# Turning the attention's output on TensorE in the last two units, and the order of the products for the new values

## The chip, the cores and the metric

One core of a Trainium2 chip runs the whole program. The metric is the device time of one execution in microseconds, as the median of several runs. The core's engines work side by side, each through an instruction list of its own: TensorE (matmuls and transposes, results into PSUM), VectorE, ScalarE, GpSimd, and SyncE, which here only issues DMAs.

## What is computed

Three steps follow each other: a linear attention whose state is corrected by a delta rule, a dense network of two layers, and a routed network with eight experts of which each token takes one.

```python
# attention: q, k, v of (4, 8, 768, 48), beta of (4, 8, 768)
for t in range(S):
    y[:, :, t] = np.einsum('bhd,bhde->bhe', q[:, :, t], state)
    v_old = np.einsum('bhde,bhd->bhe', state, kt)
    state = state + bt[:, :, :, None] * np.einsum('bhd,bhe->bhde', kt, vt - v_old)
x = y.transpose(0, 2, 1, 3).reshape(3072, 384)
# dense network
h = x @ w_in
x = np.maximum(0.01 * h, h) @ w_out
# routed network
e_idx = np.argmax(x @ w_gate + modality_bias[modality_id], axis=1)
out[mask] = gate_w[mask, None] * (np.maximum(x[mask] @ w1[e], 0.0) @ w2[e])
```

## The kernel before

**Units.** The attention is cut into 12 units, numbered `u["i"]` from 0 to 11. A unit holds 128 tokens of two batches, that is 16 heads; 6 units follow each other in time for the first two batches and 6 for the other two. Within a unit the recurrence is replaced by matrix products: `gram` multiplies keys and queries, `base` and `merge` build the inverse of a triangular 128x128 matrix for each head, and `step` takes the state through the unit. Every float32 operand is kept as two float16 halves, a high and a low one, and a product is three matmuls: high by high, high by low, low by high (`P3`).

**The inverse and the new values.** The last step of `merge`, `d2(q)`, makes the inverse of four heads: VectorE writes it as `r1`, ScalarE casts the high half `mh`, and GpSimd subtracts to get the low half `ml` (L445). `q` runs from 0 to 3, so the last piece holds heads 12 to 15. `new` in `step` multiplies the inverse by the right side `R` and gives the new values `U`: two PSUM tiles `pu`, one for the even heads (`hh` 0) and one for the odd, with 8 heads of 3 matmuls each (L495). `carry` then updates the state, and `seen` forms the unit's output: PSUM tiles `py`, from which ScalarE casts the high half of `X` and VectorE subtracts the low one (L539). Together they are the tile `x`, tokens by 384 columns for two batches and two halves.

**The dense network.** `moe1(u)` works on the 256 tokens of a unit. It needs `x` with the columns on the partitions. `turn` makes that tile, `xt` (one buffer): for unit 0 by twelve TensorE transposes into two PSUM tiles `pxt` and two VectorE copies, for all others by two DMA transposes that SyncE issues (L709). After `turn` come eight steps `up` (L724, 18 matmuls each into a PSUM tile `ph`; two such buffers, which `pxt` shares), `up2` (ScalarE and VectorE write the two halves of `gt`, L735 and L736) and `down` (L746, 12 matmuls each into `po`). The last `down` ends in `x1`, which goes to the DRAM table `x1d` (L754), and in the gate's logits `lg` (L755).

**The order.** From unit 2 on, TensorE, ScalarE, GpSimd and SyncE keep the order in which the program is written; VectorE's order is chosen by a scheduler, and so are all orders in the opening (units 0 and 1). The loop over units hands out slots: in slot `n` it runs one piece of the dense network of the unit before, then the attention's pieces of that slot. The turn of a unit is put ahead of what is still left of the unit before, which is one `down`:

```python
if n == OFF - 1:
    fs = net.moe1(U[i])
    m = fs[:1] + m + fs[1:]
```

In units 1 to 9 the slots after `seen` also hold the pieces `prod` of a unit two further on; units 10 and 11 have none.

**The end.** `route` turns the logits into table rows and scatters them (GpSimd, `tb`, L850), `plan` counts the blocks of each expert, and `block` works on 256 tokens of one expert: SyncE loads `info` and the weights `wf` (L964), GpSimd gathers the tokens `xg` from `x1d`, ScalarE and VectorE split both into halves (L625, L626), TensorE turns the tokens (`pet`, L998) and multiplies (`eh` L1009, `eo` L1024). Three blocks are planned before the last two units are counted and start as soon as unit 11's dense network is through.

Of the kernel before, what the change touches and what calls it, by code (L numbers as in the profile page):

```python
# [62 lines left out]
class Net:  # L63
# [385 lines left out]
    def step(self, u):  # L449
        nc = self.nc  # L450
# [3 lines left out]
        P3 = ((0, 0), (0, 1), (1, 0))  # L454
# [33 lines left out]
        def new():  # L488
            M, R, U = [u["mh"], u["ml"]], st["R"], st["U"]
            pu = [self.ps.tile([128, 8, 48], F32, tag="ps", name=f"pu{hh}") for hh in range(2)]  # L490
            for hh in range(2):
                for p in range(8):
                    n = 2 * p + hh
                    for i, (a, b) in enumerate(P3):
                        nc.tensor.matmul(pu[hh][:, p], M[a][n // 8][:, n % 8, :], R[b][:, n, :],  # L495
                                         start=(i == 0), stop=(i == 2))
                nc.scalar.activation(hp(U[0], hh), pu[hh], ACTF.Copy, scale=1.0 / ST)
                nc.vector.scalar_tensor_tensor(out=hp(U[1], hh), in0=pu[hh], scalar=1.0 / ST, in1=hp(U[0], hh),
                                               op0=ALU.mult, op1=ALU.subtract)
# [19 lines left out]
        def seen():  # L519
# [22 lines left out]
            u["x"] = [[X[i][:, 8 * o:8 * o + 8].rearrange("p n d -> p (n d)") for i in range(2)] for o in range(2)]  # L542

        return [old, new, carry, seen]

    def setup_moe(self):
# [152 lines left out]
    def moe1(self, u):  # L699
        nc = self.nc  # L700
        g, c = u["g"], u["c"]
        P3 = ((0, 0), (0, 1), (1, 0))
        st = {}

        def turn():
            xt = st["xt"] = self.m2.tile([128, 2, 2, 3, 128], F16, tag="xt", name="xt", bufs=1)
            if u["i"]:
                for i in range(2):
                    nc.sync.dma_start_transpose(out=xt[:, i].rearrange("p t d n -> p (t d) n"), in_=u["xx"][i])  # L709
                return  # L710
            for t in range(2):
                pt = self.pm.tile([128, 2, 3, 128], F16, tag="ph", name="pxt")
                for i in range(2):
                    for d in range(3):
                        nc.tensor.transpose(pt[:, i, d], u["x"][t][i][:, d * 128:(d + 1) * 128], self.id16)
                nc.vector.tensor_copy(xt[:, :, t], pt)

        def up(f2):
            xt = st["xt"]
            ph = self.pm.tile([128, 2, 256], F32, tag="ph", name="ph")  # L720
            for ff in range(2):
                f = 2 * f2 + ff
                for i, (a, b, d) in enumerate((a, b, d) for b in range(2) for d in range(3) for a in range(2 - b)):
                    nc.tensor.matmul(ph[:, ff], self.win[a][:, d, f * 128:(f + 1) * 128], xt[:, b, :, d, :],  # L724
                                     start=(i == 0), stop=(i == 8))
            s = SG / (SX * SW)
            tl = self.m2.tile([128, 2, 256], F32, tag="tl", name="tl")
            nc.scalar.activation(tl, ph, ACTF.Copy, scale=0.01 * s)  # L728
            nc.vector.scalar_tensor_tensor(out=tl, in0=ph, scalar=s, in1=tl, op0=ALU.mult, op1=ALU.max)  # L729
            st["t", f2] = tl  # L730

        def up2(f2):
            tl = st.pop(("t", f2))
            G = st["g", f2] = self.m2.tile([128, 2, 2, 256], F16, tag="gt", name="gt")
            nc.scalar.copy(G[:, 0], tl)  # L735
            self.pace = nc.vector.tensor_tensor(out=G[:, 1], in0=tl, in1=G[:, 0], op=ALU.subtract).ins  # L736

        def down(f2):
            if f2 == 0:
                st["po"] = [self.pm.tile([128, 392], F32, tag="po", name=f"po{t}") for t in range(2)]  # L740
            po, G = st["po"], st.pop(("g", f2))
            for ff in range(2):
                f = 2 * f2 + ff
                for t in range(2):
                    for i, (a, b) in enumerate(P3):
                        x = nc.tensor.matmul(po[t], G[:, a, ff, t * 128:(t + 1) * 128], self.wout[b][:, f, :],  # L746
                                             start=(f == 0 and i == 0), stop=(f == 15 and i == 2))
            self.pace = x.ins
            if f2 == 7:
                for t in range(2):  # L750
                    x1 = self.m2.tile([128, 392], F32, tag="x1", name="x1")
                    nc.scalar.activation(x1, po[t], ACTF.Copy, scale=1.0 / (SG * SW))
                    r = (2 * g + t) * self.S + c * 128
                    nc.sync.dma_start(out=self.x1d[r:r + 128, :], in_=x1[:, :384])  # L754
                    nc.vector.tensor_copy(self.lg[:, 2 * (g * self.NC + c) + t, :], x1[:, 384:])  # L755

        w = lambda f, x: lambda: f(x)
        none = lambda: None
        r = [(turn, none), (w(up, 0), w(up2, 0)), (w(up, 1), w(up2, 1))]
        for f2 in range(8):  # L760
            r.append((w(down, f2), none))
            if f2 < 6:
                r.append((w(up, f2 + 2), w(up2, f2 + 2)))
        return r
# [510 lines left out]
```

## Time and profile before

| | us |
|---|---|
| median of 3 runs | 969.84 (966.62 to 973.54) |
| the profiled execution | 967.95 |
| its span, first to last instruction | 966.1 |

| engine | busy us | share |
|---|---|---|
| TensorE, matmuls | 849.6 | 88% |
| TensorE, weight loads | 642.4 | 66% |
| VectorE | 732.9 | 76% |
| ScalarE | 527.1 | 55% |
| GpSimd | 531.8 | 55% |

Weight loads run beside matmuls. A share is an average over the opening, the units and the experts' blocks; what a wait costs is read at its own place. The mean granted clock of TensorE is 0.976 of full speed.

### The profile page before, as it was taken

How to read it: one execution, taken by the hardware profiler on the slowest of the kernel's cores; microseconds unless marked ns; L12 is line 12 of the kernel's file. 1: busy time of each engine (PE TensorE's matmuls, PEld its weight loads, DVE VectorE, ACT ScalarE, POOL GpSimd, SP SyncE). 2: the span in 40 equal slices, each digit the busy share in tenths (PEclk: the TensorE clock that was granted, in tenths of full speed). 3: DMA queues.
4: the chain of work that ended last, by engine and by line, in shares of the span. 5: the costliest groups of instructions: out<-in, count | busy, mean ns of one | idle time of the engine just before them, and what ended most of it. 6: DMA issues, size and time to landing. Idle time of an engine off the chain costs nothing. (4 is left out here: it accounts for less than half of the span.)

```text
span 966.1 us, 26359 instructions
## 1 busy us (share of the span) xinstructions
PE 849.6 (88%) x10914; PEld 642.4 (66%) x10914; DVE 732.9 (76%) x1391; ACT 527.1 (55%) x915; POOL 531.8 (55%) x723
## 2 busy tenths in 40 slices
PE   2555789899999999999999999898989889999994
PEld 1434667677767777777777676676767667777773
DVE  7999789786878787878878696984667766767671
ACT  4666586465645555556555554443445455665551
POOL 3537558568585868686867676652413424242321
PEclk9999998799999999999999999999999989999998
DMA  8447544235537281928281827132075567777750
GB/s 224 122 118 167 116 108 119 48 76 94 109 55 147 44 159 28 173 30 172 31 168 14 169 31 139 26 57 46 3 216 138 189 229 223 258 230 240 243 170 20
DMA packets 316501, 119.47 MB, mean 124 GB/s; under 512 B 281851, under 2 KB 298660, under 8 KB 316372
## 3 DMA queue, kind: packets, MB, share of 16 engines
q1 hardware_dynamic: 306676, 95.55, 44.3%
q10 hardware_dynamic: 5760, 12.59, 4.0%
q0 software_dynamic: 3936, 9.57, 2.8%
q8 instruction: 87, 1.43, 0.6%
q14 instruction: 42, 0.34, 0.1%
HBM read 85.99 MB, written 19.07 MB: 109 GB/s over the span
## 5 line engine op out<-in xcount | busy, mean ns | idle before, releaser
L746 PE MATMUL po<-wouth,gt 128*128 128x392 f16 x768 | 209.0, 334 | 6.4 <-DVE gt L736 6.3
L724 PE MATMUL ph<-xt,winh 128*128 128x256 f16 x1152 | 207.7, 275 | 6.7 <-DMA xt<-x 6.7
L746 PEld LDWEIGHTS <-gt 128*128 128x128 f16 x1152 | 107.9, 99 | 81.4 <-DVE gt L736 11.1
L724 PE MATMUL ph<-xt,winl 128*128 128x256 f16 x576 | 138.5, 275 | 0.0
L746 PE MATMUL po<-woutl,gt 128*128 128x392 f16 x384 | 127.9, 333 | 0.0
L724 PEld LDWEIGHTS <-winh 128*128 128x128 f16 x1152 | 113.5, 99 | 20.0 <-DMA xt<-x 2.9
L729 DVE SCALAR_TENSOR_TENSOR tl<-ph,tl 128x512 f32<-128x512 f32 x96 | 65.8, 685 | 52.9 <-ACT tl L728 52.7
L736 DVE TENSOR_TENSOR gt<-tl,gt 128x512 f16<-128x512 f32 x96 | 84.8, 883 | 21.9 <-ACT gt L735 19.5
L1009 PE MATMUL eh<-ext,wah 128*128 128x256 f16 (+1 forms) x624 | 98.5, 266 | 2.5 <-DVE ext L999 2.5
L1030 POOL DMA_INDIRECT out_dram<-ob,info x25 | 25.6, 1026 | 123.2 <-ACT ob L1029 119.2
L728 ACT ACTIVATE tl<-ph 128x512 f32<-128x512 f32 x96 | 56.9, 593 | 64.3 <-PE ph L724 63.8
L735 ACT CAST gt<-tl 128x512 f16<-128x512 f32 x96 | 59.2, 617 | 57.4 <-DVE tl L729 55.9
L279 DVE SCALAR_TENSOR_TENSOR blf<-pg,betas,up 128x256 f32<-128x256 f32 x192 | 79.6, 475 | 7.8 <-PE pg L273 7.0
L289 POOL TENSOR_TENSOR bl<-blf,bh 128x512 f16<-128x512 f32 x48 | 57.8, 1204 | 48.8 <-ACT bh L288 48.6
L1009 PE MATMUL eh<-ext,wal 128*128 128x256 f16 (+1 forms) x312 | 80.7, 266 | 0.0
L445 POOL TENSOR_TENSOR ml<-r,mh 128x512 f16<-128x512 f32 x48 | 59.7, 1252 | 18.3 <-ACT mh L444 17.9
L318 POOL TENSOR_TENSOR t<-t,tmp 128x15 f32<-128x15 f32 (+4 forms) x165 | 61.4, 372 | 12.9
L1009 PEld LDWEIGHTS <-wah 128*128 128x128 f16 x624 | 58.6, 98 | 14.9 <-issue 5.2
L1024 PE MATMUL eo<-wbh,egh 128*128 128x384 f16 (+1 forms) x200 | 66.0, 330 | 0.0
L1024 PE MATMUL eo<-wbl,egh 128*128 128x384 f16 (+1 forms) x200 | 66.0, 330 | 0.0
L1024 PE MATMUL eo<-wbh,egl 128*128 128x384 f16 (+1 forms) x200 | 66.0, 330 | 0.0
L724 PEld LDWEIGHTS <-winl 128*128 128x128 f16 x576 | 56.9, 99 | 11.6 <-issue 4.4
(324 smaller groups left out, 2166.2 us busy)
## 6 DMA issues: line engine op xcount, KB each, us to landing
wf<-in_moe_w_dram SPq DMA_DIRECT2D x52, 768.0 KB, 4.6
x<-in_moe_w_in_dram ACTq DMA_DIRECT2D x24, 256.0 KB, 3.7
x<-in_moe_w_out_dram ACTq DMA_DIRECT2D x16, 384.0 KB, 3.0
bd<-bh SPq DMA_DIRECT2D x12, 512.0 KB, 3.8
t<-td SPq DMA_DIRECT2D x12, 512.0 KB, 4.9
r<-td SPq DMA_DIRECT2D x12, 512.0 KB, 7.1
k<-in_k_dram SPq DMA_DIRECT2D x24, 192.0 KB, 3.7
q<-in_q_dram SPq DMA_DIRECT2D x24, 192.0 KB, 4.3
```

Source lines behind the costliest of these rows:

```text
L279: nc.vector.scalar_tensor_tensor(out=f[:, :, 2 * pp + hh], in0=pg[hh][:, pp], scalar=self.betas[:, c, g * 16 + n:g * 16 + n + 1], in1=self ...
L289: nc.gpsimd.tensor_tensor(out=l, in0=f[:, i], in1=h, op=ALU.subtract)
L318: eng.tensor_tensor(out=t[:, j + 1:16, 0:j + 1], in0=t[:, j + 1:16, 0:j + 1], in1=tv, op=ALU.subtract)
L445: nc.gpsimd.tensor_tensor(out=u["ml"][o][:, qs], in0=r1, in1=u["mh"][o][:, qs], op=ALU.subtract)
L724: nc.tensor.matmul(ph[:, ff], self.win[a][:, d, f * 128:(f + 1) * 128], xt[:, b, :, d, :], start=(i == 0), stop=(i == 8))
L728: nc.scalar.activation(tl, ph, ACTF.Copy, scale=0.01 * s)
L729: nc.vector.scalar_tensor_tensor(out=tl, in0=ph, scalar=s, in1=tl, op0=ALU.mult, op1=ALU.max)
L735: nc.scalar.copy(G[:, 0], tl)
L736: self.pace = nc.vector.tensor_tensor(out=G[:, 1], in0=tl, in1=G[:, 0], op=ALU.subtract).ins
L746: x = nc.tensor.matmul(po[t], G[:, a, ff, t * 128:(t + 1) * 128], self.wout[b][:, f, :], start=(f == 0 and i == 0), stop=(f == 15 and i == 2))
L1009: nc.tensor.matmul(ph[:, ff], W[a][:, d, f * 128:(f + 1) * 128], xt[:, b, d, :], start=(d == 0 and i == 0), stop=(d == 2 and i == 2))
L1024: nc.tensor.matmul(po[t], G[a][:, ff, t * P:(t + 1) * P], W[b][:, f, :], start=(f == 0 and i == 0), stop=(f == 7 and i == 2))
```

## The change

In `new`, the loop over the halves of the inverse moves outside the loop over the heads: for each of the two PSUM tiles, 16 matmuls with `mh` come first and 8 with `ml` follow. The start flag is set on the first matmul of a tile only, where before each head had one, and the stop flag on the last. In `turn`, the DMA transposes remain for units 1 to 9; units 10 and 11 take the way of unit 0, TensorE transposes and VectorE copies. Lines below the first edit are one higher in the changed kernel.

```diff
             for hh in range(2):
-                for p in range(8):
-                    n = 2 * p + hh
-                    for i, (a, b) in enumerate(P3):
-                        nc.tensor.matmul(pu[hh][:, p], M[a][n // 8][:, n % 8, :], R[b][:, n, :],
-                                         start=(i == 0), stop=(i == 2))
+                for a in range(2):
+                    for p in range(8):
+                        n = 2 * p + hh
+                        for b in range(2 - a):
+                            nc.tensor.matmul(pu[hh][:, p], M[a][n // 8][:, n % 8, :], R[b][:, n, :],
+                                             start=(p == 0 and a + b == 0), stop=(p == 7 and a == 1))
...
         def turn():
             xt = st["xt"] = self.m2.tile([128, 2, 2, 3, 128], F16, tag="xt", name="xt", bufs=1)
-            if u["i"]:
+            if 0 < u["i"] < 10:
                 for i in range(2):
                     nc.sync.dma_start_transpose(out=xt[:, i].rearrange("p t d n -> p (t d) n"), in_=u["xx"][i])
                 return
```

TensorE's list before, in unit 10, from the end of `seen` (`py`) over the last two `down` steps (`po`) to the first `up` (`ph`):

```order
L536 MATMUL py_12246<-uh,ll 128x48
L746 LDWEIGHTS gt
L746 MATMUL po_11500<-wouth,gt 128x392
...
L746 MATMUL po_11501<-wouth,gt 128x392
L724 LDWEIGHTS winh
L724 MATMUL ph<-xt,winh 128x256
```

The same place in the changed kernel, from the end of one `down` step over the twelve transposes to the next `down`:

```order
L747 LDWEIGHTS gt
L747 MATMUL po_11501<-wouth,gt 128x392
L716 LDWEIGHTS x
L716 MATMUL pxt<-id_88,x 128x128
...
L747 LDWEIGHTS gt
L747 MATMUL po_11500<-wouth,gt 128x392
```

The transposes stand between the last two `down` steps, 12 matmuls on either side; in unit 11 it is the same.

SyncE's queue before, from unit 10's turn (the first DMA_TRANSPOSE; `t` and `r` are the inverse's parts for unit 11) to the first load of a plan (`ei`):

```order
L329 DMA r_12054<-td_399 128x16x128
L709 DMA_TRANSPOSE xt<-x 128x6x128 x2
L176 DMA v<-in_v_dram 128x8x48 x2
L754 DMA x1d<-x_12383 128x384
L754 DMA x1d<-x_12387 128x384
L709 DMA_TRANSPOSE xt<-x 128x6x128 x2
L754 DMA x1d<-x_13259 128x384
L754 DMA x1d<-x_13263 128x384
L947 TENSOR_LOAD ei_13294
```

And in the changed kernel:

```order
L329 DMA r_12054<-td_399 128x16x128
L176 DMA v<-in_v_dram 128x8x48 x2
L755 DMA x1d<-x_12397 128x384
L755 DMA x1d<-x_12401 128x384
L755 DMA x1d<-x_13287 128x384
L755 DMA x1d<-x_13291 128x384
L948 TENSOR_LOAD ei_13322
```

Four transposes are gone from the queue, and nothing else in it has moved.

VectorE's list before, in unit 11, from the second low half of `X` (L539) to the first routing step on the new logits (L796; the rows between are constants of the routing):

```order
L539 SCALAR_TENSOR_TENSOR x<-py_13131,x 128x8x48
L838 TENSOR_TENSOR r_off<-r_off,cnt 128x8
L883 TENSOR_SCALAR p_pick<-io_404 1x8
L896 TENSOR_SCALAR p_val<-io_404 1x8
L925 TENSOR_SCALAR p_tk<-iok 1x19
L755 COPY lg<-x_13259 128x8
L755 COPY lg<-x_13263 128x8
L796 TENSOR_TENSOR r_l<-lg,biast 128x16
```

And in the changed kernel:

```order
L540 SCALAR_TENSOR_TENSOR x<-py_13145,x 128x8x48
L839 TENSOR_TENSOR r_off<-r_off,cnt 128x8
L884 TENSOR_SCALAR p_pick<-io_404 1x8
L897 TENSOR_SCALAR p_val<-io_404 1x8
L926 TENSOR_SCALAR p_tk<-iok 1x19
L717 COPY xt<-pxt 128x2x384 x2
L756 COPY lg<-x_13287 128x8
L756 COPY lg<-x_13291 128x8
L797 TENSOR_TENSOR r_l<-lg,biast 128x16
```

The two copies of the turned tile stand ahead of the logits; the rest keeps its order. In unit 10 they stand directly behind the two L540.

## Rows read from the trace of the kernel before

**Rows 1.** The page, part 1: busy time, share of the span, instructions

```profile
PE 849.6 (88%) x10914; PEld 642.4 (66%) x10914; DVE 732.9 (76%) x1391; ACT 527.1 (55%) x915; POOL 531.8 (55%) x723
```

**Rows 2.** Who waited for whom, whole run: total us, times, longest

```profile
PE pu L495 <- POOL ml L445: 7.1, 12, 1.4
...
PE ph L724 <- DMA xt<-x: 6.7, 2, 4.2
```

**Rows 3.** Timeline, TensorE, unit 10: start, us, what [idle before <-releaser]

```profile
649.11 0.33 PE L746 MATMUL po<-wouth,gt 128*128 128x392 f16 x1
...
657.46 0.37 PE L724 MATMUL ph<-xt,winh 128*128 128x256 f16 x1 [4.22 <-DMA xt<-x]
...
660.94 0.63 PE L356 MATMUL px<-t,bm 128*128 128x64 f16 x16
661.41 0.27 PE L724 MATMUL ph<-xt,winh 128*128 128x256 f16 x1
...
663.37 0.40 PE L365 MATMUL pz<-xp,r 128*128 128x64 f16 x8
```

**Rows 4.** Windows: PE, PEld, DVE, ACT, POOL busy, PEclk, DMA share, GB/s

```profile
656.00:662.00 6.00, 4.54 (x40) 3.46 (x40) 0.17 (x1) 0.80 (x2) 0.00 (x0) 0.72 0.58 120
...
709.00:739.00 30.00, 30.00 (x236) 22.13 (x235) 21.48 (x46) 15.68 (x23) 7.35 (x8) 1.00 0.70 210
```

**Rows 5.** Timeline, TensorE, unit 11

```profile
698.50 0.33 PE L746 MATMUL po<-wouth,gt 128*128 128x392 f16 x1
...
705.16 0.39 PE L724 MATMUL ph<-xt,winh 128*128 128x256 f16 x1 [2.53 <-DMA xt<-x]
...
712.63 0.33 PE L746 MATMUL po<-wouth,gt 128*128 128x392 f16 x1
```

**Rows 6.** Timeline, VectorE: the low halves of X in units 10 and 11

```profile
649.96 1.01 DVE L539 SCALAR_TENSOR_TENSOR x<-py,x 128x384 f16<-128x384 f32 x2
...
700.16 0.56 DVE L539 SCALAR_TENSOR_TENSOR x<-py,x 128x384 f16<-128x384 f32 x1
```

**Rows 7.** Transposes on TensorE: the experts' (timeline), unit 0's (line and tile views)

```profile
730.51 0.33 PE L998 MATMUL pet<-id,exh 128*128 128x128 f16 x3
...
731.18 0.27 PE L724 MATMUL ph<-xt,winh 128*128 128x256 f16 x1
...
L715 PE MATMUL pxt<-id,x x12: 219/219/314, 120.9 to 121.7; 128*128 128x128 f16 x12
...
L716 DVE COPY xt<-pxt x2: 547/552/558, 121.8 to 122.3; 128x768 f16<-128x768 f16 x2
```

**Rows 8.** Timeline, the wait for the last piece of ml before unit 10's new values

```profile
642.31 1.16 POOL L445 TENSOR_TENSOR ml<-r,mh 128x512 f16<-128x512 f32 x1 [0.32 <-ACT mh L444]
...
643.53 0.20 PE L495 MATMUL pu<-r,ml 128*128 128x48 f16 x1 [0.16 <-POOL ml L445]
```

**Rows 9.** Who waited for whom, TensorE, from 100 to 150 us (unit 0)

```profile
PE pu L495 <- POOL ml L445: 3.3, 4, 1.4
```

**Rows 10.** Timeline, unit 11: ScalarE, VectorE and TensorE towards the last down

```profile
714.82 0.62 ACT L735 CAST gt<-tl 128x512 f16<-128x512 f32 x1 [1.23 <-PE po L746]
...
736.36 0.69 DVE L736 TENSOR_TENSOR gt<-tl,gt 128x512 f16<-128x512 f32 x1 [0.74 <-ACT gt L735]
...
739.12 0.38 PE L1009 MATMUL eh<-ext,wah 128*128 128x256 f16 x2
```

**Rows 11.** Waits and timeline: the loads of the first expert's weights

```profile
SPq L947 <- DVE e_c L771: 0.5, 1, 0.5
...
704.07 0.18 DVE L771 TENSOR_SCALAR e_c<-r_l 128x32 f32<-128x32 f32 x1
...
706.04 2.33 SPq L964 DMA_DIRECT2D wf<-in_moe_w_dram  x4
...
715.34 1.48 ACT L625 ACTIVATE wah<-wf 128x1536 f16<-128x1536 f32 x1
```

**Rows 12.** The chain that ended last, its last gather

```profile
767.02 7.68 DMA xg<-x1d,idx
```

## The prediction

> **What bounds the kernel now.** I read the page first: TensorE is busy 849.6 us, 88% of the span, and no other engine passes 76% [rows 1]. So the question is where TensorE stands still in the two places that the diff touches, and whether the end of the program follows it. The waits of TensorE show both places by name [rows 2]: `up` waits 6.7 us for the transposed `xt`, in two waits only, and the products of `new` wait 7.1 us in 12 waits for the low half `ml` that GpSimd makes.
>
> The timeline shows the two waits for `xt`. In unit 10 the `down` matmuls start at 649.11 and end at 653.24; then TensorE is idle for 4.22 us, until 657.46 [rows 3]. In unit 11 the idle time is 2.53 us, before 705.16 [rows 5]. Units 1 to 9 show no such wait; there the matmuls of `gram` stand between. The idle time has a tail: the 18 matmuls of the first `up` of unit 10 take 657.46 to 660.94, 3.48 us, and the 18 of the next take 661.41 to 663.37, 1.96 us [rows 3]. The granted clock says why: 0.72 on average from 656 to 662, against 1.00 from 709 to 739 [rows 4]; it lay at the lower level (1.2 GHz) after the idle stretch and then rose to 2.4 GHz.
>
> **The turn of unit 10.** The four DMA transposes leave SyncE's queue; 24 TensorE transposes and 4 copies on VectorE come in. On TensorE they stand between the last two `down` steps. Twelve transposes of the same shape and type (L998) take 730.51 to 731.18, 0.67 us [rows 7]. Twelve `down` matmuls take half of 649.11 to 653.24 less a tail, 2.0 us. So: `down` 6 ends at 649.11 + 2.0 = 651.1. The low half of X is written from 649.96 for 1.01 us, to 650.97 [rows 6], so the transposes find their input and end at 651.8. `down` 7 ends at 653.8. Meanwhile VectorE copies the two PSUM tiles in 0.55 us each [rows 7], done by about 653.0, under `down` 7. If that cover were gone, 1.2 us would show. `up` starts at 653.8 instead of 657.46: **3.65 us**. Without the idle time the clock should not fall: another 3.48 - 1.96 = **1.5 us**. Unit 10 gives 5.15 us, and the work behind it in this unit hangs on TensorE and shifts with it.
>
> **The turn of unit 11.** `down` 6 runs 698.50 to 700.5 [rows 5]. Here VectorE is later: the second low half runs 700.16 to 700.72 [rows 6], so TensorE waits some 0.3 us, with 12 `down` matmuls queued behind the waiting transpose; whoever needs their results (ScalarE for `x1`, VectorE for the logits) gets them 0.9 us later than now. Transposes to 701.4, `down` to 703.4, `up` at 703.4 instead of 705.16: 1.75 us. The three `up` steps take 705.16 to 712.63, 7.47 us, against 3 x 1.96 = 5.88: 1.6 us for the clock. That makes 3.35 us on TensorE alone.
>
> Not all of it lasts. From the third `up` on, ScalarE and VectorE run one chain of `gt` and of the first expert's weights, with hardly a gap: ScalarE's cast at 714.82 follows `down`, and the last `gt` is ready at 736.36 + 0.69 = 737.05 [rows 10]. TensorE needs it 12 matmuls (2.0 us) before 739.12, at 737.1. There is 0.1 us of room, so TensorE can be no earlier than this chain. Its front is held by VectorE's small routing steps, which start on logits that are now 0.9 us later; stepping those rows on by hand I estimate the chain 3.0 us earlier, not 3.35. A second hold: SyncE waits for one of these steps (L771, at 704.07) before it issues the weights at 706.04, four loads at once; ScalarE casts the first at 715.34 without having waited [rows 11]. In unit 11's own time the cast is wanted 3 us earlier and the load is issued 0.9 us later. I take 0.3 us for it. Unit 11 gives **2.7 us**; bounds 0 and 3.35.
>
> **The new values.** All 16 products with `mh` now precede the 8 with `ml` in each half. One unit shows the place: TensorE waits 0.16 us until 643.53, for the last of four pieces of `ml`, which GpSimd starts at 642.31 [rows 8]. That piece belongs to the last four heads, whose first `ml` product was the 21st matmul of its half and is now the 23rd. So only 2 matmuls, some 0.025 us apart, move ahead of the wait, and 2 instead of 4 are left behind it: 0.05 us a unit. Of the 7.1 us, 3.3 in 4 waits lie in unit 0 [rows 9], where the scheduler mixes the two halves and TensorE waits for VectorE directly after. The other eight waits at 0.05 us: **0.4 us**, and 0 to 1.3 as bounds (the upper one if each wait shrinks by the 0.15 us of six matmuls). The start flag is now set once for a PSUM bank; that has no instruction of its own. The order of ScalarE's and VectorE's steps in the opening changes at two places by an instruction or three, which I cost at nothing, plus or minus 0.5 us.
>
> **What lies behind.** The end follows TensorE: after 739.12 the chain goes over the last `down`, the logits, the routing, the table and the last gathers, as the one at 767.02 that takes 7.68 us [rows 12]. Each of these starts on a result of the step before, not at a fixed time, so I let the whole gain through. SyncE is spared the issue of four transposes ahead of `v` and `x1d`; no wait for these shows, so I count nothing.
>
> **Sum.** 5.15 + 2.7 + 0.4 = 8.25 us. The profiled execution took 967.95 us (its span is 966.1), so it would take 959.7. The median of the three timed runs is 969.84, 1.9 us above it, and less 8.25 gives 961.6. I take the point between, a base of 968.9, and predict 960.6 us, 0.85% less.
>
> **Rivals.** (a) *The weights or VectorE hold unit 11.* The load for the cast at 715.34 lands some time before that; if it lands just before, nearly 3 us of unit 11 are given back, and unit 10's 5.15 and 0.4 are left: 963.3 us. For it speaks that four loads are issued together; against it that the first had 9.3 us to land [rows 11].
>
> (b) *The transposes are dear or don't keep the clock up.* The only transposes of this kind in the trace (L715, unit 0) start between 120.9 and 121.7 and last 0.22 us: 1.0 us for twelve, 0.35 more than I took [rows 7]. If the clock fell after them as it does now after the wait, both tails of 1.5 us would stay. Then 3.65 + 1.75 - 0.7 + 0.4 = 5.1 us and 963.8. Against it: twelve L998 transposes took 0.67 us in a stretch with clock 1.00 [rows 4, 7]. The Trainium skill, page "TensorE: Matmul & The Clock Gate", section "Part 4: PE-mode transpose", speaks for it: it gives about 275 ns for one transpose inside a kernel and says that transposes do not count as activity for the clock. An estimate from that page is 12 x 0.275 = 3.3 us a unit, which would leave some 3 us of the sum; the rows of L998 do not agree with it.
>
> (c) *Slower: TensorE stands before the transposes.* They stand in TensorE's own order now, with `down` behind them. If VectorE's X came later by d, all of TensorE would be d later, where the DMA let it go on. Today X is ready 0.1 us before TensorE arrives in unit 10 and 0.2 us after in unit 11 [rows 6]. The change breaks even when d is about 4 us in both units; at 6 us the time would be about 973. VectorE's order has only one `gt` subtraction and a few small steps ahead, so I see no source for 4 us.
>
> (d) *More than I count.* If `new` gives its upper bound, unit 11 its 3.35 and the later stretches close up as well, 10.3 us are saved: 958.6.
>
> **How the numbers follow.** Forecast 65% (959 to 962.5), (a) 15%, (b) 7%, (c) 3%, (d) 10%. Medians of this kernel scatter by some 0.3% (its three runs span 966.62 to 973.54), and about 1% is what can be told from no change. The 1% line lies at 9.7 us saved: (d) is beyond it, and scatter puts about a third of the forecast and a tenth of (a) and (b) there. That is 0.34 faster by over 1%, 0.62 within, 0.04 slower. The range for 8 in 10 takes in (a), (b), (d) and half a percent of scatter at either end: 954 to 968.
>
> **What the profile after would show.** No wait for DMA `xt` in units 10 and 11; transposes of about 0.67 us between the two `down` steps; clock 1.00 through both `up` steps; from the start of `down` 6 to the start of `up` 4.7 us in unit 10 (now 8.35) and 4.9 in unit 11 (now 6.66); `new`'s waits smaller by 0.05 us, not gone. I am wrong if TensorE shows a wait of over 1 us before the transposes or before the first expert's weights, or if the wait before the last gather grows by what was won.

## The result, and the profile after

Over 17 runs of each kernel the median went from 972.96 us to 965.16 us; the ratio is 0.991, with a 95% interval of 0.9887 to 0.9934. The medians lie 7.8 us apart; by the ratio it is 8.75 us less (6.4 to 11), where the sum was 8.25. Two of its terms did not go as they were written, though, and the step from the turn to the end held only in some of the traces.

The profiled execution of the changed kernel took 967.48 us (span 965.8), while that of the kernel before took 967.95. The two traces are 0.5 us apart where the medians are about 8 us apart, so the traces are read stretch by stretch here, not by their ends. One reason shows at once: at the start of unit 10's `down` 6, ahead of the first turn that was changed, the changed kernel's trace is already 3.23 us behind (652.34 against 649.11). Over all the traces of this document this start lies between 646.39 and 653.41 us; what makes it differ was not looked into. The page of the changed kernel, part 1, answers to [rows 1]:

```profile
PE 851.7 (88%) x10938; PEld 643.0 (67%) x10938; DVE 735.1 (76%) x1395; ACT 526.5 (55%) x915; POOL 534.6 (55%) x723
```

TensorE has 24 instructions more, VectorE four. The timeline of TensorE in unit 10 of the changed kernel, to be laid beside [rows 3]:

```profile
652.34 0.33 PE L747 MATMUL po<-wouth,gt 128*128 128x392 f16 x1
...
654.32 0.83 PE L716 MATMUL pxt<-id,x 128*128 128x128 f16 x12
...
654.99 0.33 PE L747 MATMUL po<-wouth,gt 128*128 128x392 f16 x1
...
656.98 0.27 PE L725 MATMUL ph<-xt,winh 128*128 128x256 f16 x1
...
658.95 0.63 PE L356 MATMUL px<-t,bm 128*128 128x64 f16 x16
```

No bracket stands behind `ph`: the wait of 4.22 us is gone. The twelve transposes take 654.32 to 654.99, 0.67 us. From the start of `down` 6 to the first `up` it is 4.64 us (forecast 4.7, before 8.35), and the first `up` takes 1.97 us to the work behind it (before 3.48). The same for unit 11, to be laid beside [rows 5]:

```profile
697.47 0.33 PE L747 MATMUL po<-wouth,gt 128*128 128x392 f16 x1
...
699.46 0.83 PE L716 MATMUL pxt<-id,x 128*128 128x128 f16 x12
...
702.12 0.27 PE L725 MATMUL ph<-xt,winh 128*128 128x256 f16 x1
...
708.24 0.33 PE L747 MATMUL po<-wouth,gt 128*128 128x392 f16 x1
```

Here it is 4.65 us to the first `up` (forecast 4.9, before 6.66), and the three `up` steps take 6.12 us (before 7.47). VectorE's copies of the turned tile, from the timeline, start under the last `down`:

```profile
654.86 1.02 DVE L717 COPY xt<-pxt 128x768 f16<-128x768 f16 x2 [0.73 <-PE pxt L716]
...
699.99 1.02 DVE L717 COPY xt<-pxt 128x768 f16<-128x768 f16 x2 [0.17 <-PE pxt L716]
```

They end at 655.88 and 701.01, 1.1 us before `up` wants them. The windows over both stretches (TensorE, its weight loads, VectorE, ScalarE, GpSimd busy, then the granted clock) answer to [rows 4]:

```profile
650.00:662.00 12.00, 12.00 (x232) 9.86 (x226) 6.04 (x13) 5.44 (x12) 7.12 (x7) 1.00 0.19 38
703.00:745.00 42.00, 41.93 (x332) 31.40 (x330) 33.02 (x101) 22.33 (x30) 12.45 (x12) 1.00 0.64 191
```

TensorE is busy for all 12 us of the first and the clock stays at 2.4 GHz (1.00, where 0.72 stood). For `new`, who waited for whom on TensorE, first in unit 0 (100 to 150 us, [rows 9] before), then from 150 to 700 us:

```profile
PE pu L496 <- ACT mh L444: 2.9, 2, 2.3
PE pu L496 <- POOL ml L445: 0.5, 1, 0.5
...
PE pu L496 <- POOL ml L445: 3.2, 4, 0.8
PE pu L496 <- ACT mh L444: 1.0, 4, 0.3
```

In unit 0, 3.4 us stand where 3.3 stood. Behind it, 4.2 us stand where [rows 2] less [rows 9] leave 3.8. The short waits are gone; four longer ones remain, each split into 0.3 us for `mh` and 0.8 for `ml`.

What unit 11 won did not stay, though. TensorE starts the first expert's matmuls (`eh`) at 734.74, 4.38 us before [rows 10]; at the second expert's first matmuls only 0.97 us of this lead are left. The timeline of the second expert's gather in the changed kernel shows where it went (GpSimd issues the gather `xg` in two parts, VectorE splits weights in `wal`, ScalarE casts the gathered tokens in `exh`):

```profile
739.58 1.69 DVE L627 SCALAR_TENSOR_TENSOR wal<-wf,wah 128x1536 f16<-128x1536 f32 x1
739.77 2.43 POOL L983 DMA_INDIRECT xg<-x1d,idx  x1 [5.51 <-ACT egh L1014]
...
742.50 1.96 POOL L983 DMA_INDIRECT xg<-x1d,idx  x1 [0.30 <-issue]
...
747.09 0.52 ACT L626 ACTIVATE exh<-xg 128x384 f16<-128x384 f32 x1 [2.34 <-DMA xg<-x1d,idx]
...
750.12 0.52 ACT L626 ACTIVATE exh<-xg 128x384 f16<-128x384 f32 x1 [2.51 <-DMA xg<-x1d,idx]
```

The first part starts 0.19 us after a split has begun and takes 2.43 us. In the trace before, it started at 743.93, 0.04 us ahead of the split, and took 1.05 us; the second part took 1.28:

```profile
743.93 1.05 POOL L982 DMA_INDIRECT xg<-x1d,idx  x1 [5.44 <-ACT egh L1013]
743.97 1.75 DVE L626 SCALAR_TENSOR_TENSOR wal<-wf,wah 128x1536 f16<-128x1536 f32 x1
...
745.29 1.28 POOL L982 DMA_INDIRECT xg<-x1d,idx  x1 [0.30 <-ACT wah L625]
```

The gather started 4.16 us earlier than there, and its last tokens were cast only 0.97 us earlier. Added up, the changed kernel's trace was 3.23 us behind at unit 10, won 5.22 us there, lost 0.96 us on the way to unit 11, won 3.35 us by the first `eh` and lost 3.41 us at the second expert: 0.97 us. The chain that ended last shows the third expert's gather as it was, to be laid beside [rows 12]:

```profile
766.09 7.65 DMA xg<-x1d,idx
```

Two questions were left for experiments: what each part of the change is worth, and whether the lead is lost by chance or always.

### The profile page after: what moved, and what is told of

Same layout as the page of the kernel before. It is cut to its first block, busy times and chain, and to the rows that moved or that the text cites. A ratio compares the mean times of both kernels' runs of the same rounds, so it can differ in the third digit from the quotient of the medians.

```text
span 965.8 us, 26397 instructions
## 1 busy us (share of the span) xinstructions
PE 851.7 (88%) x10938; PEld 643.0 (67%) x10938; DVE 735.1 (76%) x1395; ACT 526.5 (55%) x915; POOL 534.6 (55%) x723
## 5 line engine op out<-in xcount | busy, mean ns | idle before, releaser
L725 PE MATMUL ph<-xt,winh 128*128 128x256 f16 x1152 | 204.7, 273 | 0.1
L725 PE MATMUL ph<-xt,winl 128*128 128x256 f16 x576 | 136.3, 273 | 0.0
L318 POOL TENSOR_TENSOR t<-t,tmp 128x15 f32<-128x15 f32 (+4 forms) x165 | 63.6, 386 | 12.9
L444 ACT CAST mh<-r 128x512 f16<-128x512 f32 x48 | 29.5, 617 | 61.1 <-DVE r L442 61.1
```

Of the source, the lines that this page charges most:

```text
L318: eng.tensor_tensor(out=t[:, j + 1:16, 0:j + 1], in0=t[:, j + 1:16, 0:j + 1], in1=tv, op=ALU.subtract)
```

## The experiments

Fourteen traces bear on the explanation. The table puts them side by side; its numbers are differences of start times in the timelines. "Unit 10" is the time from `down` 6 to the second `up`, "unit 11" from `down` 6 to the `down` behind three `up` steps. "Gather to split" is the start of the second expert's gather on GpSimd less that of the VectorE split nearest to it; the two times behind it are how long the gather's parts took to issue. The lead is how much earlier than in the first trace TensorE began the first, second and third expert's `eh` (for the third, the step that stands at 785.94 there). A lead also holds what a trace had won or lost ahead of unit 10, so compare the three leads within a row, not one lead between rows.

| kernel, trace | unit 10 | unit 11 | gather to split, parts | third `idx` | lead at 1st, 2nd, 3rd |
|---|---|---|---|---|---|
| before, first | 12.30 | 14.13 | -0.04: 1.05, 1.28 | 1.87 | 0 |
| before, second | 11.90 | 15.81 | -0.20: 1.05, 1.37 | 1.87 | -1.5, -1.5, -1.5 |
| order in `new` alone | 11.24 | 15.10 | -0.10: 1.05, 1.27 | 0.23 | -1.2, -1.2, 4.9 |
| unit 11 alone | 12.07 | 10.99 | -0.29: 1.05, 1.45 | 0.23 | 1.1, 1.5, 7.5 |
| unit 10 alone | 7.94 | 11.66 | -0.20: 1.05, 1.37 | 0.23 | 2.6, 2.7, 8.7 |
| turn alone | 7.94 | 10.99 | +0.31: 2.30, 1.96 | 0.23 | 5.6, 3.0, 9.2 |
| changed, first | 7.08 | 10.77 | +0.19: 2.43, 1.96 | 1.87 | 4.4, 1.0, 0.7 |
| changed, second | 7.08 | 10.77 | -0.41: 1.05, 1.58 | 1.87 | 8.3, 8.7, 8.8 |
| split one slot later | 7.08 | 10.76 | -0.92: 1.05, 2.17 | 1.87 | 10.3, 8.6, 8.4 |
| transposes last | 8.09 | 11.76 | -0.25: 1.05, 1.42 | 1.87 | 6.8, 7.2, 7.0 |
| split two slots later | 7.08 | 10.77 | -1.84: 1.06, 0.97 | 1.88 | 7.9, 7.4, 6.8 |
| all units turned | 7.08 | 10.76 | -0.48: 1.05, 1.65 | 1.87 | 4.5, 4.9, 5.2 |
| both tiles' `mh` first | 7.08 | 10.77 | -0.53: 1.05, 1.70 | 1.87 | 10.0, 10.5, 9.9 |
| third split later | 7.08 | 10.77 | -0.31: 1.05, 1.49 | 0.23 | 11.1, 11.6, 14.6 |

**The turn alone.** The kernel before with the second edit only:

```diff
-            if u["i"]:
+            if 0 < u["i"] < 10:
```

> The kernel before with the second edit alone: units 10 and 11 are turned on TensorE, the products of new keep their old order. Theory (the sum: unit 10 5.15, unit 11 2.7 to 3.35, new 0.4): 7.8 to 8.5 us less than before, ratio 0.9912 to 0.9919; from the start of the next to last down to the first up 4.65 us in both units, no wait for xt. Rival 1 (the order in new carries the change, in units that no row of the two traces shows): less than 4 us here, ratio above 0.996. Rival 2 (the turn is worth the whole, and new is worth nothing or costs): 8.75 us or more, ratio 0.991 or less. In the trace, where its last gather lands decides how much of the 8 us is left at the end: theory 8, rival 3 (the last experts' gathers do not follow) 4 to 5.

Measured: 960.01 us against 966.84 for the kernel before, ratio 0.9938 (0.9912 to 0.9964), 6.0 us. The theory's 0.9912 to 0.9919 lies at the edge of the interval; rival 1 (above 0.996) lies at the other edge, with 0.9964 as the end of the interval, and the second (0.991 or less) is just outside. The trace speaks against rival 1: with the turn alone, units 10 and 11 take 7.94 and 10.99 us (before 12.30 and 14.13). In this trace rival 3 was at work: of a lead of 5.6 us, 3.0 were left at the second expert, whose gather met a split (timeline):

```profile
738.36 1.69 DVE L626 SCALAR_TENSOR_TENSOR wal<-wf,wah 128x1536 f16<-128x1536 f32 x1
...
738.67 2.30 POOL L982 DMA_INDIRECT xg<-x1d,idx  x1 [5.63 <-ACT egh L1013]
```

Unit 10 took 7.94 us instead of 7.08 here. ScalarE stood 1.27 us before it cast the second half of X, VectorE's low half came later by that, and TensorE waited in the middle of the transposes (timeline of the same trace):

```profile
650.04 0.49 ACT L538 ACTIVATE x<-py 128x384 f16<-128x384 f32 x1 [1.27 <-remote]
...
651.17 0.68 PE L715 MATMUL pxt<-id,x 128*128 128x128 f16 x9 [0.25 <-DVE x L539]
```

This is the forecast's rival (c) at a small scale: X came about 1.3 us later, and `down` and `up` behind the transposes came 0.86 us later with it.

**The order in `new` alone.** The kernel before with the first edit only (the diff of the change, its first part).

> The kernel before with the first edit alone: in new, all products with the high half stand ahead of those with the low half; the turn is left to the DMA in units 10 and 11. Theory: 0.4 us less (0 to 1.3), ratio 0.9987 to 1.0; TensorE's waits for ml before the new values sum to 6.5 to 7 us, against 7.1. Rival 1 (the order carries the change): 3 us or more, ratio 0.997 or less. Rival 2 (the order costs, since the 1.1 to 3 us that the changed kernel's trace had lost by unit 10 came from it): 1 to 3 us more, ratio 1.001 to 1.003.

Measured: 965.36 us, ratio 0.9983 (0.9962 to 1.0003), 1.6 us less with an interval that takes in zero and 0.4. Rival 2 (1.001 or more) is outside, and the 3 us of rival 1 lie inside the interval but near its end. TensorE's waits for `ml` before `new` sum to 3.8 us in this trace, well under the theory's 6.5 to 7, but 4.4 us of waits for `mh` have come in, where none were. Together that is 8.2 us against 7.1: 4.1 in unit 0 and 4.1 behind it. So the waits give no gain; they have moved from `ml` to `mh`, which the theory had not foreseen.

**Unit 10 alone, and unit 11 alone.**

```diff
-            if u["i"]:
+            if u["i"] not in (0, 10):
```

(and 11 in the other kernel).

> The kernel before with unit 10 alone turned on TensorE. Theory: 5.15 us less, ratio 0.9947; in the trace from the start of the next to last down to the first up 4.65 us in unit 10 and 6.7 in unit 11, the first up 2.0 us in unit 10 and the three ups 7.5 in unit 11. Rival (the work that stands behind in this unit, above all the low halves of the inverse from GpSimd, holds a part of it): 3 us or less, ratio 0.997 or more.

> The kernel before with unit 11 alone turned on TensorE. Theory: 2.7 us less, at most 3.35, ratio 0.9965 to 0.9972; in the trace 8.35 us from the start of the next to last down to the first up in unit 10, 4.65 in unit 11, and the first expert's matmuls stand 3 us earlier. Rival (the first expert's weights, or the chain of ScalarE and VectorE, hold the end): under 1 us, ratio 0.999 or more.

Measured: unit 10 alone 961.22 us, ratio 0.9941 (0.9925 to 0.9958), 5.7 us; unit 11 alone 963.22 us, ratio 0.9972 (0.9946 to 0.9998), 2.7 us. Both theories hold. For unit 10 the rival (0.997 or more) is outside the interval. For unit 11 the rival (0.999 or more) still lies inside its upper end, and the trace decides: `down` 6 starts at 700.57, 2.07 us behind the first trace, and the first `eh` at 738.05, 1.07 us ahead of it, so the 3.14 us won in unit 11 are all there at the first expert. In the traces the wait for the DMA is less steady than the one trace before had shown: in the four traces with a DMA turn, unit 10 takes 11.24 to 12.30 us and unit 11 takes 11.66 to 15.81, where the TensorE turn takes 7.08 (or 7.94) and 10.77 (or 10.99) each time.

**The kernel before and the changed one again**, on one chip, with a second trace of each.

> The kernel before once more, for a second trace beside those of this chip. Theory A (where the gathers of the second and third expert land is decided by when they fall against VectorE's splits of the weights, wal, not by the turn): if idx of the third gather takes 0.23 us and not 1.87, the span is about 960 us and no 4.8 us wait stands before the last transposes; if it takes 1.87, the span is about 966 as in the first trace. Theory B (the late gather belongs to the kernel): the wait of 4.8 us and the 7.7 us gather are there again in any case.

> The changed kernel once more, on one chip with the two that follow. Theory A: the first gather of the second expert starts 0.1 to 0.4 us after the split wal and takes about 2.4 us instead of 1.05, and 2 to 3.4 us of what units 10 and 11 gave are lost there; the ratio is 0.991 to 0.994. Theory B (the whole 8.25 us goes through, and the loss in the first trace was chance): the lead at the first expert's matmuls is still there at the second's, ratio 0.990 to 0.992.

Measured: the kernel before 969.66 us in its profiled run, third `idx` 1.87 us, a wait of 4.9 us before the last transposes. The changed kernel 961.56 us, ratio 0.9926 (0.9896 to 0.9955). Its gather started 0.41 us ahead of the split this time and took 1.05 us (timeline):

```profile
735.30 1.05 POOL L983 DMA_INDIRECT xg<-x1d,idx  x1 [5.09 <-ACT wah L626]
...
735.71 1.70 DVE L627 SCALAR_TENSOR_TENSOR wal<-wf,wah 128x1536 f16<-128x1536 f32 x1
```

The lead at the first expert's matmuls, 8.3 us, was still there (8.7 and 8.8) at the second's and the third's. So neither expectation held as written: the collision of theory A is not there in each execution, and theory B's chance is a matter of 0.2 us in the start of the gather. Of the traces with the second expert's splits in their old place, the two in which the gather starts after the split lose 2.6 and 3.4 us of their lead; in all others it starts 0.04 to 0.53 us ahead and nothing is lost, although the gather's second part still falls into the split there and takes 1.27 to 1.70 us (0.97 when it is free).

**The split one slot later.** An added line in `block`:

```diff
+        if k == 1 and plan is self.plan0:
+            pre = {0: [gather], 1: [w(cut, "a", 0)], 2: [w(cut, "a", 1)], 4: [w(cut, "b", 0), halves],
+                   6: [w(cut, "b", 1), turn]}
```

> The changed kernel with the second expert's first weights split one slot later, so that VectorE has no wal to do when GpSimd issues this expert's gather. Theory A (a GpSimd gather that starts inside a wal stands until the wal ends): both gathers take 1.0 to 1.5 us instead of 2.4 and 2.0, the second high half exh starts 2 to 3 us earlier against the first expert's matmuls, TensorE has no wait before the second expert's transposes, and the time is 2 to 3 us less than the changed kernel's. Theory B (the gather is slow for another reason, such as the weights' loads that run beside it): its duration stays above 2 us or its landing stays late, and the time does not change.

Measured: 959.85 us, ratio 0.9911 (0.9877 to 0.9944), not to be told from the changed kernel's. The splits moved by too little. The gather's first part was free, its second fell into them (timeline):

```profile
733.98 1.05 POOL L983 DMA_INDIRECT xg<-x1d,idx  x1 [5.66 <-ACT egh L1014]
...
734.90 3.43 DVE L627 SCALAR_TENSOR_TENSOR wal<-wf,wah 128x1536 f16<-128x1536 f32 x2
...
735.33 2.17 POOL L983 DMA_INDIRECT xg<-x1d,idx  x1 [0.30 <-issue]
```

1.7 us of the lead were lost, so the remedy missed and the mechanism got another instance.

**The transposes last.** They stand behind the last `down`, with nothing to cover VectorE's copies:

```diff
-                        m = fs[:1] + m + fs[1:]
+                        m = m + fs if U[i]["i"] >= 10 else fs[:1] + m + fs[1:]
```

> The changed kernel with the transposes of units 10 and 11 behind the last down instead of ahead of it, so that VectorE's copies lie open. Theory (working of unit 10: the cover of the last down is worth up to 1.2 us): TensorE waits 0.8 to 1.2 us before the first up in each unit, from the start of the next to last down to the first up 5.4 to 5.9 us instead of 4.65, and the clock stays at 1.00 since the wait is short: 1.6 to 2.4 us more in all by unit 11's end. Rival (a short wait also brings the clock down, as the long one did): each unit gives back another 1.5 us, 4.5 to 5.5 us in all, and the first up takes 3.5 us.

Measured: 960.94 us, ratio 0.9926 (0.9899 to 0.9953). The first `up` of unit 10 in the timeline of its trace, and the window around it:

```profile
654.20 0.27 PE L725 MATMUL ph<-xt,winh 128*128 128x256 f16 x1 [0.85 <-DVE xt L717]
...
650.00:662.00 12.00, 11.15 (x130) 8.69 (x128) 5.84 (x12) 4.28 (x8) 4.83 (x5) 1.00 0.40 67
```

The wait is 0.85 us, it is 5.66 us from `down` 6 to `up` in each unit, 1.0 us more than in the changed kernel, and the granted clock stays at 1.00. The theory holds; the rival's second tail did not come. The runs cannot tell 2 us.

**The split two slots later.** As the last but one, with `a` 0 in slot 2 and `a` 1 in slot 3.

> The changed kernel with the second expert's first weights split two slots later (the run before moved them by one slot, 0.9 us, and its second gather fell into the split and took 2.17 us). Theory A: no wal runs while GpSimd issues the second expert's two gathers, both take 1.0 to 1.6 us, TensorE stands under 0.3 us before the second expert's transposes and first matmuls, and the lead won by unit 11 is the same at the second expert's matmuls as at the first's; the median is 0 to 3 us below the changed kernel's. Theory B (the split is not what holds the gather): one of the two gathers takes over 2 us although no wal runs, or the second high half lands as late.

Measured: 960.85 us, ratio 0.9945 (0.9917 to 0.9973). Both parts are free now (timeline):

```profile
735.50 1.06 POOL L983 DMA_INDIRECT xg<-x1d,idx  x1 [4.94 <-DMA x1d<-x]
736.86 0.97 POOL L983 DMA_INDIRECT xg<-x1d,idx  x1 [0.30 <-DVE e_p L822]
...
737.34 1.75 DVE L627 SCALAR_TENSOR_TENSOR wal<-wf,wah 128x1536 f16<-128x1536 f32 x1
```

Theory A holds for the gather; B is out. But the lead falls from 7.9 to 7.4 us at the second expert, where it rose by 0 to 0.4 us in the traces with a free first part and the old slots. TensorE waits 0.87 us before the second expert's `eh` for VectorE's `ext`, which comes behind splits that now end later (0.21 us in the changed kernel's second trace). So the later splits cost 0.5 to 0.9 us themselves, and the median shows no gain.

**All units turned on TensorE.**

```diff
-            if 0 < u["i"] < 10:
+            if u["i"] < 0:
```

> The changed kernel with all units turned on TensorE, also units 1 to 9, where no row shows TensorE waiting for the DMA. Theory (the price of the turn by the row of 0.67 us for twelve transposes, with VectorE's copies under other matmuls): 0.67 to 0.85 us more in each of nine units, 6 to 7.6 us in all against the changed kernel, ratio to the kernel before 0.997 to 1.0. Rival 1 (the transposes are dear, 0.275 us each): 3.3 us in each unit, 30 us in all, ratio above 1.015. Rival 2 (the DMA transposes hold something else in these units, so sparing them wins): less than 3 us more than the changed kernel, ratio 0.994 or less.

Measured: 959.92 us, ratio 0.9924 (0.9897 to 0.9951). On the same chip the kernels with split two slots later and with both tiles' `mh` first had 960.85 and 960.14. The group of transposes in the trace, busy us and mean ns:

```profile
L716 PE MATMUL pxt<-id,x 128*128 128x128 f16 x144 | 10.4, 224 | 0.0
```

A price of 3.3 us a unit (rival 1) is out, and so is the theory's ratio of 0.997 to 1.0. In the trace TensorE is 4.4 us later than in the changed kernel's second trace at `new` of unit 9 and 3.6 us at the third expert, less than the theory's 6 to 7.6 (3.1 us at `new` of unit 9 against the first trace); and the median shows no price at all, as rival 2 said. What the nine spared DMA turns give back was not found.

**Both tiles' high half first.**

```diff
-            for hh in range(2):
-                for a in range(2):
+            for a in range(2):
+                for hh in range(2):
...
+            for hh in range(2):
```

The last line is the loop over the two casts, which now stand behind all products.

> The changed kernel with the products of new in the order all high half of both tiles, then all low half of both: 32 matmuls instead of 16 ahead of the first low one. Theory (only the matmuls that stand ahead of the wait for the last piece of ml shorten it, 0.025 us each): the waits for ml in units 3 to 6 (1.1 us in the changed kernel's trace) vanish, but the first tile is finished 0.4 us later, and its cast with it; together minus 1 to plus 1 us, no difference that can be measured, ratio 0.990 to 0.9935. Rival (new is where more is to be won, since 7.1 us of waits stood there before): 3 us or more less than the changed kernel, ratio below 0.988.

Measured: 960.14 us, ratio 0.9939 (0.9916 to 0.9963), no difference that can be measured. From 150 to 700 us TensorE's waits before `new` are shorter, but not gone:

```profile
PE pu L496 <- POOL ml L445: 1.7, 4, 0.4
PE pu L496 <- ACT mh L444: 0.9, 4, 0.3
```

The 16 matmuls that moved ahead take 0.4 us off the `ml` wait in four units (0.8 to 0.4). That is the rule by which `new` was costed, 0.025 us a matmul. The waits for `mh` stay. The rival (3 us or more) is out.

**The third split later.** In most traces the third expert's `idx` meets a split too. A last kernel moves that one:

```diff
+        if k == 2 and plan is self.plan0:
+            pre = {0: [gather, w(cut, "a", 0)], 4: [w(cut, "a", 1), halves], 5: [w(cut, "b", 0)],
+                   6: [w(cut, "b", 1), turn]}
```

> The changed kernel with the third expert's second piece of the first weights split two slots later, after its gather has been issued. In five of the traces without ScalarE's stalls idx (GpSimd) takes 1.87 us because it meets this split, the gather behind it lands 7.7 us after its issue, and TensorE stands 4.6 to 4.8 us before the last of the planned transposes; in the four traces of one chip it takes 0.23 us, the landing 3.3 us, and TensorE does not stand. Theory A (the split holds idx, and that sets when the gather lands): idx 0.23 us, the gather's second part issued 1.6 us earlier and landed 4 to 6 us earlier, no wait over 0.5 us before these transposes, and 4 to 6 us less than the changed kernel: ratio to the kernel before 0.985 to 0.988. Theory B (the landing is late because of the loads beside it): idx 0.23 us, but the landing still 5 us or more after the second issue, and at most 2 us less than the changed kernel, ratio above 0.989.

Measured: 956.2 us against 967.6 for the kernel before, ratio 0.9897 (0.9867 to 0.9928): the lowest time and ratio of the study, 10 us less than before. The interval reaches from theory A's range to B's, and the changed kernel was not run on this chip, so the trace decides. First the timeline of the same place in the changed kernel's second trace, then that of this kernel:

```profile
754.60 1.87 POOL L978 TENSOR_SCALAR idx<-info 128x2 int32<-128x2 int32 x1
754.66 1.74 DVE L627 SCALAR_TENSOR_TENSOR wal<-wf,wah 128x1536 f16<-128x1536 f32 x1
...
758.29 2.39 POOL L983 DMA_INDIRECT xg<-x1d,idx  x1 [0.30 <-issue]
...
766.15 0.52 ACT L626 ACTIVATE exh<-xg 128x384 f16<-128x384 f32 x1 [5.49 <-DMA xg<-x1d,idx]
```

```profile
751.78 0.23 POOL L978 TENSOR_SCALAR idx<-info 128x2 int32<-128x2 int32 x1
...
753.85 0.97 POOL L983 DMA_INDIRECT xg<-x1d,idx  x1 [0.30 <-issue]
...
754.82 1.76 DVE L627 SCALAR_TENSOR_TENSOR wal<-wf,wah 128x1536 f16<-128x1536 f32 x1 [0.68 <-ACT wah L626]
...
757.00 0.52 ACT L626 ACTIVATE exh<-xg 128x384 f16<-128x384 f32 x1 [0.89 <-DMA xg<-x1d,idx]
...
763.83 0.56 PE L1010 MATMUL eh<-ext,wah 128*128 128x256 f16 x2 [2.56 <-DVE ext L1000]
```

`idx` takes 0.23 us, the gather's second part is cast 3.2 us after its issue instead of 7.9, and TensorE has no wait before the transposes, where it had 4.9 us. Theory A holds for the gather. A new wait of 2.56 us follows, though: the delayed splits now stand ahead of VectorE's copies (`ext`). Of the lead, 11.6 us at the second expert's first matmuls and 17.0 at its last `down`, 14.6 are left at the third's: 3.0 us won, less than the 4 to 6 of theory A.

## Why the prediction came out as it did

**Unit 10** was right: 12.30 less 7.08 is 5.22 us against 5.15, with both of its parts (3.71 for the wait, 1.51 for the clock). The price of the transposes was the L998 row's, 0.67 us, and the clock stayed at 1.00 over and behind them, so rival (b) is out. The Trainium skill, page "TensorE: Matmul & The Clock Gate", section "Part 4: PE-mode transpose", gives about 275 ns for one transpose inside a kernel. The traces come near that for one (224 ns on average in the L716 row), but twelve overlap, and the estimate of 3.3 us, twelve times the page's figure, was wrong for that reason. Whether transposes count as activity for the clock, no run here shows. What one trace could not tell is that the DMA's wait varies: over four traces unit 10 took 11.88 us on average, which makes the gain 4.8.

**Unit 11** came out on TensorE (3.36 us against 3.35) partly by luck, since its two parts missed in opposite directions: `up` came 2.01 us earlier against `down` 6 instead of 1.75, and the three `up` steps gave 1.35 us instead of 1.6. The 0.3 us of waiting for X did not come: the first six transposes need only the first half of X, which was ready. In what lasts the term was mis-sized. I took 0.65 us off, for ScalarE's and VectorE's chain to the last `gt` and for the weights' load. The last `gt` started at 732.12 us instead of 736.36, 4.2 us earlier, and the lead grew by 3.35 us from `down` 6 (1.03) to the first `eh` (4.38). VectorE's routing step was indeed later against `down` 6 (6.24 us behind it instead of 5.57), but it did not hold the chain: ScalarE's cast behind the third `up` already came at 710.43 instead of 714.82. So nothing had to be taken off, and rival (a) did not come.

**The new values**, 0.4 us: the term is not shown. Matmuls ahead of the wait do shorten it by 0.025 us each, but I looked at `ml` alone. The first product with the last piece of `mh` was the 19th of its half and is now the 13th, six matmuls or some 0.15 us earlier, and up to 0.3 us of waits for ScalarE stand where none were. In the pair of traces the sum is 0.5 us worse, in the second trace of the changed kernel 0.6 us better behind unit 0 (3.2 instead of 3.8) and 1.6 us worse in it (4.9 instead of 3.3). The measured 1.6 us of the edit alone has an interval of -0.3 to 3.7 us. At `new` of unit 10 the five traces with the old order stand at 641.77 to 643.77 us, and seven with the change's order (all units turned left aside) at 640.04 to 645.91, so the traces show no gain either. Whether the edit is worth anything stays open.

**"I let the whole gain through"** is the step that failed in part. It holds in the changed kernel's second trace and in four others with the old slots, and it fails where the second expert's gather starts a few tenths of a microsecond too late, at a cost of 2.6 to 3.4 us. I had named something near it ("if the wait before the last gather grows by what was won"), but as a sign to look for, without a mechanism and for another gather: the last one took 7.65 us against 7.68. What the rows show is this: a GpSimd instruction that meets a VectorE split of two SBUF operands takes until that split is over, plus most of its own 1.05 us (739.58 + 1.69 = 741.27, and the gather ends 0.93 us later; 738.36 + 1.69 = 740.05, and 0.92). In the twelve traces with the old slots the gather starts 4.1 to 4.9 us after SyncE issues the store of `x1d`, the split 4.6 to 4.7 us after it, so which comes first is open in each execution. What varies is the landing of the store: in the seven traces that show it, its second part lands 2.8 to 3.7 us after its issue, and the gather starts 0.81 or 0.82 us after the landing in each. The Trainium skill, page "SBUF — State Buffer", section "SBUF: two separate sides", has the rule: VectorE and GpSimd share a pair of ports, and of a VectorE instruction with two SBUF inputs and a GpSimd one that reads SBUF, whichever starts first holds the pair to its end. The traces agree, with one difference in the order: `idx` began 0.06 us ahead of the split (754.60, 754.66) and was held nevertheless.

The sum came out because the terms' errors were small against the two large ones, and by some luck: 0.65 us too much was taken off for unit 11, 0.4 us were put down for `new` that no run shows, and a loss of 2.6 to 3.4 us that only some executions have was not counted. How many of the 17 runs had it is not known. The time itself, 965.16, lies 4.6 us above the 960.6 that I gave since the kernel before, too, came out higher in these runs (972.96) than the base of 968.9.

## What to carry to other kernels

A transfer that TensorE waits for costs its wait and, where the granted clock fell, the time at the lower level behind it. Both can be read off a timeline, but take a second trace, since the wait varied here from one to the next; turning twelve 128x128 blocks on TensorE under work that was there anyway cost 0.67 us against 5. When a stage is moved by some microseconds, look up what runs beside each GpSimd instruction behind it, since a gather that met a VectorE split of two SBUF operands lost 2.6 to 3.4 us here, more than many edits win. And when two single traces differ by half a microsecond and the medians by eight, compare stretches and take a second trace of both.

## What the runs showed of the hardware that was not expected

Waits of 0.85 us (transposes last) and 1.62 us (unit 10 alone, before unit 11's first `up`, at 704.09) on TensorE left its granted clock at 1.00; one of 2.56 us (third split later) brought it to 0.72 in the window from 762 to 768, as the one of 4.22 us had; the lower level is 1.2 GHz.

From its issue to the cast, the second part of the third gather took 3.2 us where SyncE's weight loads were issued behind it (third split later), and 7.9 us where they were issued while GpSimd was still held (changed kernel, second trace). That these loads are the cause was not tried apart.

On one chip, all four traces (the order in `new` alone, unit 11 alone, unit 10 alone, the turn alone) show ScalarE standing for 1.2 to 2.6 us before a `tl` of unit 11 and for 1.7 us before the second `egh` of the second expert, three of them also for 1.3 us before X in unit 10, with a releaser that the profile calls remote. None of the other ten traces shows one. In these four the third expert's split starts 3.4 us behind the one before it instead of 2.7, after `idx` has begun and ended, so that the third gather is free and the lead grows by 6 us from the second expert to the third. It looks as if the second of the stalls makes the program shorter; this was not tried apart. What ScalarE waits for was not found.
